# Rows for the w2-gradient tiles: five in turn, then half rows, and a new home for the second x tile

## The chip, the cores and the metric

The kernel runs on one core of a Trainium2 chip. The metric is the device time of one execution in microseconds. Three runs of the kernel before gave 1481.81, 1483.12 and 1483.87 us; the median is 1483.12 us. The engines of the core are TensorE (PE, with its weight loads PEld), VectorE (DVE), ScalarE (ACT), GpSimd (POOL) and SyncE (SP). Each works through its own list of instructions in order and waits on semaphores for the others. SyncE and GpSimd also start the transfers; a list entry that waits holds back all that stand behind it, transfers included.

## The reference

The computation is one block of a network and the gradients of all its inputs. With x of 2048 x 1024, a condition c and a modulation matrix w_mod:

```
mod = silu(c) @ w_mod                    # six rows: sa, ca, ga, sb, cb, gb
h   = layernorm(x) * (1 + ca) + sa
x   = x + ga * irfft2(rfft2(h) * (w_r + 1j*w_i))
h   = layernorm(x) * (1 + cb) + sb
x   = x + gb * (gelu(layernorm(h) @ w1 + b1) @ w2 + b2)
out, vjp = x, gradients of x, w_r, w_i, w1, b1, w2, b2, c, w_mod for grad_out
```

w1 is 1024 x 3584, w2 is 3584 x 1024, everything is stored in bfloat16, and the ten outputs are the block's value and nine gradients. The gradient of w2 (`out_6`, 3584 x 1024) is the product of the hidden activations, transposed, with the gradient that reaches the second matrix product.

## The kernel before

The two-dimensional transform is done as dense products with cosine and sine matrices that the kernel makes itself. Folding (sums and differences of mirrored rows and columns) cuts the transform into four classes CE, SE, CO and SO. The same function, `spectral_core`, serves the forward pass and the gradient: `s_fwd` makes four tiles U (products `pu`, line 471); eight `pair` steps (products `pcs`, line 504) form the spectrum, multiply it by the weights and fill R; `s_inv` makes four tiles V from R (products `pv`, line 564); and four blocks of products `po` (line 629) give the tiles `ct`, each of which is handed to `consume`.

Between the two spectral passes stand the forward products of the feed-forward part (`pp`, `pz`, `pbo`) and the gradient `pg` of its input, in four token blocks.

The part that the change touches runs from about 970 us to the end. TensorE's order there is written out by hand. A generator, `pieces()`, gives out the products of the w2 gradient (`gw2_product`, line 1073: 16 matmuls, one 128 x 512 half of a 128 x 1024 row tile, 28 row tiles `fc` in all) and then those of the w1 gradient (line 1240). `fill(n)` takes n of them. Row tiles 0 and 1 are done in the last block of the loop above, 2 to 7 are taken by `fill(2)` and `fill(10)` ahead of the spectral pass, and four halves stand beside each of the eight pairs; the rest go between the `consume` steps. Both spectral parts and fillers share the engines that empty the accumulators.

Each finished half of a w2-gradient tile is cast by whichever of VectorE and ScalarE the scheduler chooses (`nc.any`, line 1069; ScalarE for 54 of the 56) into one of the two rows of the tile `gwo`, row `fc % 2`. After the second half the row is stored by GpSimd (line 1071). So a cast of row tile `fc` waits for the store of row tile `fc - 2`. The accumulators of these products are four banks of PSUM (`ps_f`); `pu`, `pv` and part of the other spectral products have two banks (`ps_s`).

Beside the pairs run the steps of `gmod_ring` (lines 968 to 992): rows of w_mod are loaded by SyncE, reduced by VectorE (line 987), and overwritten with a row of the w_mod gradient (line 989) which GpSimd stores (line 990). Each pair loads its weights with two plain transfers (line 489) and two gathers on GpSimd (line 490) and its saved spectrum (line 492), and stores its part of the weight gradients with two plain transfers (line 550) and two scatters on GpSimd (line 551).

`consume_bwd` (line 1159) unfolds a `ct` tile, loads the matching block of x with `load_tok` (one plain transfer on SyncE, line 128, and two gathers on GpSimd, line 131), normalizes it on ScalarE (`norm_act`, line 461), and forms the gradient of x. The x tiles `xt` of the four blocks take two homes in turn (line 619), `sma` and `smb`. In both passes, `smb` also holds the matrices of CO and SO that the last two `s_inv` steps read, so the second x tile can be loaded only after those. A "home" is a tag of the pool `reg` with one buffer: a new tile of the same tag waits until the last reader of the tile before it is done. The home `gm` holds a small identity tile before the w2 products, and from pair 1 on the matrices `gm`; the home `px0` holds the pairs' evacuated tiles `cs`, and after the spectral pass of the gradient a small tile `sr`.

Ahead of the code stands only the line that sets the two homes, which the change replaces:

```
xts = [reg.tile([P, 4, D], BF16, name="xt", tag=tg)[:] for tg in ("sma", "smb")]
```

Of the kernel before, what the change touches and what calls it, by code (L numbers as in the profile page):

```python
# [11 lines left out]
BF16 = mybir.dt.bfloat16  # L12
# [5 lines left out]
P = 128  # L18
S = 2048
D = 1024  # L20
# [4 lines left out]
KH = D // 2  # L25
# [10 lines left out]
def kernel(  # L36
# [24 lines left out]
    nc = tc.nc  # L61
# [4 lines left out]
    reg = ctx.enter_context(tc.tile_pool(name="reg", bufs=1))  # L66
# [410 lines left out]
    def spectral_core(fwd, fb, sms, em, css, pt, evac_u, evac_c, evac_v, consume, o4tag, pfs=None, fill=lambda n: None, mid=lambda: None, beside=lambda n: None):  # L477
# [112 lines left out]
        for par in range(2):  # L590
            for m in range(4):
# [9 lines left out]
                if par == 0 and m > 0:  # L601
                    v = 0 if fwd else 1
                    if m == 1:
                        gm = reg.tile([P, 12, 256], BF16, name="gm", tag="gm")
# [3 lines left out]
                    else:  # L608
                        cl = (CE, SE)[m - 2]
                        for h in range(2):  # L610
                            with tc.issue_after(ld_in[0].ins):
                                nc.sync.dma_start_transpose(out=gm[:, 2 * cl:2 * cl + 2, h * P:(h + 1) * P],
                                                            in_=d_E[:, v, 2 * cl + h, :])
# [2 lines left out]
        with tc.issue_after(r_in[0].ins):  # L616
            nc.vector.tensor_scalar(out=gm[:, 8:12, :], in0=gm[:, 4:8, :], scalar1=-1.0, scalar2=None, op0=ALU.mult)
        ct = reg.tile([P, 4, 4, D], BF16, name="ct", tag=o4tag)
        xts = [reg.tile([P, 4, D], BF16, name="xt", tag=tg)[:] for tg in ("sma", "smb")]
        for i in range(4):  # L620
            o4 = ct[:, 3 * (i % 2)]
            for cl in range(4):
# [98 lines left out]
    def consume_fwd(i, o4, tmp, tmp2, x4):  # L721
# [13 lines left out]
        nc.sync.dma_start(out=chunk_rows(d_n3, i), in_=tmp)  # L735

    spectral_core(True, fbuf, (smA, smB), em1[:, 1], [css[:, 0], css[:, 1]], new_pair_temps(PXT[2:6]),
                  act_copy, act_copy, act_copy, consume_fwd, "fr")

# [185 lines left out]
    for g in range(7):  # L925
        wtile = reg.tile([P, 4, D], BF16, name=f"w1T_{g}", tag=W1T[g])
        for k in range(4):
            fc = g * 4 + k
# [127 lines left out]
        halves_sum(acc3[1], p4, b == 0, b == 3)  # L1056

    gwo = reg.tile([P, 2, D], BF16, name="gwo", tag="ph")

    def hh_of(fc):  # L1060
        return hh_f[:, fc] if fc < 2 else hh_s[hh_o[fc]]
# [3 lines left out]
                         start=(t == 0), stop=(t == NT - 1))  # L1065

    def gw2_out(acc, fc, h):
        with tc.high_priority():
            nc.any.tensor_copy(out=gwo[:, fc % 2, h * KH:(h + 1) * KH], in_=acc[:])  # L1069
        if h == 1:  # L1070
            nc.gpsimd.dma_start(out=out_6[fc * P:(fc + 1) * P, :], in_=gwo[:, fc % 2])

    def gw2_product(fc, h):
        acc = ps_f("gw2acc")
        for t in range(NT):
            gw2_mm(acc, fc, h, t)
        gw2_out(acc, fc, h)
# [122 lines left out]
    def pieces():  # L1200
# [18 lines left out]
        for fc, h, acc in last:  # L1219
            gw2_out(acc, fc, h)  # L1220
# [55 lines left out]
    def beside_bwd(n):  # L1276
        for k in range(4):
            fill(1)
            if 3 - k < (1, 2, 2, 2, 2, 2, 3, 3)[n]:
                with tc.issue_after(hh_in[0].ins):  # L1280
                    next(rows34)

    spectral_core(False, fbuf2, (smA2, smB2), em2, [css2[:, 0], css2[:, 1]],
                  new_pair_temps(["t0", "t1", "t2", "t3"]), act_copy, s_copy, act_copy, consume_bwd, "fr", pfs, fill, mid_bwd, beside_bwd)

# [55 lines left out]
```

## Time and profile before

| what | value |
|---|---|
| median of three runs | 1483.12 us |
| profiled execution: its time | 1487.43 us |
| profiled execution: its span, first to last instruction | 1485.5 us |
| TensorE busy | 1402.2 us, 94% |
| VectorE busy | 1069.0 us, 72% |
| ScalarE busy | 720.3 us, 48% |
| GpSimd busy | 362.6 us, 24% |
| mean granted TensorE clock | 0.98 of full speed |
| w2-gradient casts on ScalarE | 54, mean 583 ns |
| w2-gradient stores on GpSimd | 28 of 256 KB, median 571 ns to issue |
| `pu` products of the gradient pass | 1029.81 to 1068.43 us |
| pairs of the gradient pass, first `pcs` to first `pv` of CO | 1068.43 to 1214.27 us |

All times of instructions count from the start of the span. A line of the timeline gives start, duration, engine, line of the code, operation, the tile written and the tiles read, how many instructions were merged, and in brackets how long the engine sat idle before and what released it. A line of the waits gives who waited for whom, the total, how many times, and the longest. Engines other than the one that sets the end may be idle at no cost; what counts is the wait that ends last at each place.

### The profile page before, as it was taken

The numbers are of one execution on the slowest core, as the hardware profiler recorded it, in microseconds if no ns is written. First come the engines' busy times: TensorE is split into PE (matmuls) and PEld (weight loads), VectorE is DVE, ScalarE is ACT, GpSimd is POOL, SyncE is SP. The second block draws the span as 40 slices with busy tenths as digits, with TensorE's granted clock in tenths as the row PEclk, the third lists the DMA queues.
The fourth block names the chain that finished last, engine by engine and source line by source line (L and its number), as shares of the span: only waits on it lengthen the run. The fifth ranks groups of instructions, "written<-read, shape, count | busy, mean of one in ns | idle before, by whom it ended". The sixth has DMA issues, their size and how long they took to land.

```text
span 1485.5 us, 18204 instructions
## 1 busy us (share of the span) xinstructions
PE 1402.2 (94%) x6703; PEld 653.7 (44%) x6835; DVE 1069.0 (72%) x1574; ACT 720.3 (48%) x960; POOL 362.6 (24%) x421
## 2 busy tenths in 40 slices
PE   5889989999899999999999999997999999899998
PEld 2434545444344444444344444443444444444443
DVE  5883786898799788887420899986367677888533
ACT  4765546857886756666202333332522444453211
POOL 5620541211113122212111001112134421322323
PEclk8999999999999999999999999999999999999999
DMA  9982563899776876797898266477499977565994
GB/s 335 274 226 61 150 224 122 267 245 338 252 237 213 260 241 219 236 275 230 237 290 253 97 218 227 145 209 196 127 210 246 261 229 213 161 198 154 267 222 169
DMA packets 358046, 324.27 MB, mean 218 GB/s; under 512 B 209066, under 2 KB 300736, under 8 KB 357702
## 3 DMA queue, kind: packets, MB, share of 16 engines
q1 hardware_dynamic: 324166, 207.71, 51.9%
q0 software_dynamic: 33792, 115.40, 22.5%
q8 instruction: 53, 0.87, 0.2%
q14 instruction: 35, 0.29, 0.1%
HBM read 162.06 MB, written 111.20 MB: 184 GB/s over the span
## 4 chain that ended last, share of the span: by engine, by line
PE 32%; DVE 31%; issue 16%; DMA 9%; ACT 8%; POOL 4%; SPq 0%; POOLq 0%; DVEq 0%; ACTq 0%
PE pbo L846 9%; PE pz L797 5%; DVE ct L173 5%; DVE gt L173 4%; PE pu L471 4%; PE pg L943 3%; PE gw2acc L1064 3%; PE pv L564 3%; DVE got L1027 2%; DMA out_dram<-otl 2%; PE gw1acc L1240 1%; ACT ct L461 1%; PE pp L679 1%; DVE st L437 1%; DVE w2sA L817 1%
## 5 line engine op out<-in xcount | busy, mean ns | idle before, releaser
L679 PE MATMUL pp<-gBoT,wt 128*128 128x512 bf16 x878 | 197.4, 381 | 6.4 <-DMA wt<-in_B_w_dram 2.8
L1240 PE MATMUL gw1acc<-gzh,n3n 128*128 128x512 bf16 x876 | 195.2, 381 | 1.2 <-issue 0.2
L943 PE MATMUL pg<-w1T,gzr 128*128 128x512 bf16 x876 | 194.6, 379 | 1.6 <-ACT gn3b L951 0.2
L797 PEld LDWEIGHTS <-w 128*128 128x128 bf16 x896 | 87.6, 98 | 112.5 <-issue 9.0
L679 PEld LDWEIGHTS <-wt 128*128 128x128 bf16 x896 | 88.0, 99 | 110.8 <-issue 6.0
L1240 PEld LDWEIGHTS <-n3n 128*128 128x128 bf16 x896 | 87.7, 98 | 105.7 <-issue 2.5
L943 PEld LDWEIGHTS <-gzr 128*128 128x128 bf16 x896 | 86.8, 98 | 107.9 <-issue 4.9
L797 PE MATMUL pz<-n3Ta,w 128*128 128x512 bf16 x437 | 99.5, 383 | 6.1 <-ACT gt L800 4.1
L1064 PE MATMUL gw2acc<-gB,hhsA 128*128 128x512 bf16 x438 | 99.5, 384 | 3.4 <-DMA hhsA<-d_hh 2.1
L797 PE MATMUL pz<-n3Tb,w 128*128 128x512 bf16 x439 | 98.4, 379 | 0.5
L846 PEld LDWEIGHTS <-hhA 128*128 128x128 bf16 x608 | 59.6, 99 | 74.5 <-issue 5.8
L806 ACT ACTIVATE gt<-gt 128x2048 bf16<-128x2048 bf16 x28 | 53.5, 1910 | 70.9 <-DVE gt L173 70.9
L800 ACT ACTIVATE gt<-pz,b_col 128x512 bf16<-128x512 f32 x112 | 72.8, 684 | 29.1 <-PE pz L797 27.1
L1244 ACT CAST gwo<-gw1acc 128x512 bf16<-128x512 f32 x53 | 30.8, 584 | 115.4 <-PE gw1acc L1240 96.6
L173 DVE TENSOR_TENSOR gt<-gt,gt 128x2048 bf16<-128x2048 bf16 x56 | 68.5, 1223 | 21.6 <-ACT gt L808 20.9
L1069 ACT CAST gwo<-gw2acc 128x512 bf16<-128x512 f32 x54 | 29.9, 583 | 110.9 <-DMA out_dram<-gwo 75.6
L173 DVE TENSOR_TENSOR ct<-ct 128x2048 bf16<-128x2048 bf16 x64 | 75.8, 1219 | 10.7 <-ACT ct L632 8.8
L1064 PEld LDWEIGHTS <-hhsA 128*128 128x128 bf16 x448 | 44.0, 99 | 56.4 <-DMA hhsA<-d_hh 3.8
L987 DVE CUSTOM_DVE_ANT_0 otl<-otl 128x1024 bf16<-128x1024 bf16 x24 | 29.0, 1223 | 51.7 <-DMA otl<-in_w_mod_dram 45.3
L802 ACT ACTIVATE gt<-gt 128x2048 bf16<-128x2048 bf16 x28 | 53.4, 1907 | 0.6
L808 ACT ACTIVATE gt<-gt 128x2048 bf16<-128x2048 bf16 x28 | 53.4, 1907 | 0.5
L1245 POOL DMA_DIRECT2D out_dram<-gwo x56 | 30.7, 550 | 79.6 <-ACT gwo L1244 59.3
(313 smaller groups left out, 2508.5 us busy)
## 6 DMA issues: line engine op xcount, KB each, us to landing
gzr<-d_gz SPq DMA_DIRECT2D x28, 512.0 KB
wblk<-in_w_mod_dram SPq DMA_DIRECT2D x12, 1024.0 KB
out_dram<-otl POOLq DMA_DIRECT2D x48, 256.0 KB
d_ph<-pho POOLq DMA_DIRECT2D x21, 512.0 KB
d_hh<-hhA POOLq DMA_DIRECT2D x19, 512.0 KB
w2sD<-in_B_w_dram SPq DMA_DIRECT2D x14, 512.0 KB
hhC<-d_ph SPq DMA_DIRECT2D x14, 512.0 KB
w2sA<-d_ph SPq DMA_DIRECT2D x14, 512.0 KB
```

The costliest lines, as they stand in the source:

```text
L173: return nc.vector.tensor_tensor(out=out, in0=a, in1=b, op=op)
L471: last_pu[0] = nc.tensor.matmul(pu[:], lhsT=fb[:, i, cl, c8 * P:(c8 + 1) * P], rhs=sm[:, i, :], start=(i == 0), stop=(i == 3))
L679: last_pe[0] = nc.tensor.matmul(pp[:], lhsT=wt[:, fg % 2, cch, k * P:(k + 1) * P], rhs=gBoT[j][:, cch, :], start=(cch == 0), stop=(cch == ...
L797: last_pe[0] = nc.tensor.matmul(pz[:], lhsT=w1s[g][:, cch, k * P:(k + 1) * P], rhs=n3T[:, cch, :], start=(cch == 0), stop=(cch == NDC - 1))
L800: nc.scalar.activation(out=zb[:, k, :], in_=pz[:], func=ACT.Identity, bias=b1_col[:, fc:fc + 1], scale=1.0)
L802: nc.scalar.activation(out=av, in_=zb, func=ACT.Square)
L806: nc.scalar.activation(out=sg, in_=bv, func=ACT.Sigmoid, scale=2.0 * GK)
L808: nc.scalar.activation(out=bv, in_=bv, func=ACT.Sigmoid, scale=-2.0 * GK)
L846: last_pe[0] = nc.tensor.matmul(pbs[i][:], lhsT=hh[:, k, i * P:(i + 1) * P], rhs=wp[:, k, :], start=False, stop=(g == 6 and k == 3))
L943: last_pg[0] = nc.tensor.matmul(pgs[i][:], lhsT=gzs[b, g][:, k, i * P:(i + 1) * P], rhs=w1Ts[g][:, k, h * KH:(h + 1) * KH], start=(g == 0 ...
L1064: nc.tensor.matmul(acc[:], lhsT=hh_of(fc)[:, t, :], rhs=gBs[t // 4][:, t % 4, h * KH:(h + 1) * KH], start=(t == 0), stop=(t == NT - 1))
L1240: nc.tensor.matmul(acc[:], lhsT=n3ns[t // 4][:, t % 4, cch * P:(cch + 1) * P], rhs=gz2[t // 8][:, t % 8, :], start=(t == 0), stop=(t == NT ...
```

## The change

There are three edits. First, the row tiles 0 to 7, those ahead of the pairs, take five rows in turn instead of two: the two rows of `gwo` and three rows of a new tile `gwoE` in the home `gm`. Second, from row tile 8 on, the two rows of `gwo` stay in use, but each half is stored on its own as soon as it is cast, 128 KB each. Third, the second x tile of both spectral passes has the home `px0` in place of `smb`, so that it waits for the last pair's `cs` tile to be read instead of for the last `s_inv`.

```diff
         ct = reg.tile([P, 4, 4, D], BF16, name="ct", tag=o4tag)
-        xts = [reg.tile([P, 4, D], BF16, name="xt", tag=tg)[:] for tg in ("sma", "smb")]
+        xts = [reg.tile([P, 4, D], BF16, name="xt", tag=tg)[:] for tg in ("sma", "px0")]
...
     gwo = reg.tile([P, 2, D], BF16, name="gwo", tag="ph")
+    gwoE = reg.tile([P, 3, D], BF16, name="gwoE", tag="gm")
+    gwo5 = [gwo[:, 0], gwo[:, 1]] + [gwoE[:, k] for k in range(3)]
...
     def gw2_out(acc, fc, h):
+        row = gwo5[fc % 5] if fc < 8 else gwo[:, fc % 2]
+        half = slice(h * KH, (h + 1) * KH)
         with tc.high_priority():
-            nc.any.tensor_copy(out=gwo[:, fc % 2, h * KH:(h + 1) * KH], in_=acc[:])
-        if h == 1:
-            nc.gpsimd.dma_start(out=out_6[fc * P:(fc + 1) * P, :], in_=gwo[:, fc % 2])
+            nc.any.tensor_copy(out=row[:, half], in_=acc[:])
+        if fc >= 8:
+            nc.gpsimd.dma_start(out=out_6[fc * P:(fc + 1) * P, half], in_=row[:, half])
+        elif h == 1:
+            nc.gpsimd.dma_start(out=out_6[fc * P:(fc + 1) * P, :], in_=row)
```

The scheduler's lists of the other engines follow from it. TensorE's list is as before. GpSimd's has 20 stores more, and the gathers of the second x tile of the gradient pass stand ahead of the last pair's scatters rather than behind them. On ScalarE the four normalizations of that tile come ahead of the copies of the last 16 `pv` products rather than among the `ct` casts, and one cast of a w2-gradient half goes from ScalarE to VectorE in pair 7.

## The prediction

> **What bounds the kernel now.** I read the page's busy shares first, then TensorE's waits from 960 us on, where the changed code runs, and then ScalarE, GpSimd and VectorE in order of time at the places those waits named. TensorE is busy 94% of the span; the change leaves its order of instructions as it is, so the change can only remove or add TensorE waits. The page, then TensorE's waits:
>
> ```profile
> span 1485.5 us, 18204 instructions
> PE 1402.2 (94%) x6703; PEld 653.7 (44%) x6835; DVE 1069.0 (72%) x1574; ACT 720.3 (48%) x960; POOL 362.6 (24%) x421
> ```
>
> ```profile
> PE pu L471 <- ACT U L642: 7.7, 1, 7.7
> PE po L629 <- DVE ct L632: 7.3, 2, 5.3
> PE pv L564 <- ACT V L642: 2.1, 1, 2.1
> PE gw2acc L1064 <- DMA hhsA<-d_hh: 2.1, 1, 2.1
> PE gw2acc L1064 <- ACT gwo L1069: 0.9, 2, 0.7
> ```
>
> The longest is one wait of 7.7 us for ScalarE to empty a bank of `pu`, at 1031.65 to 1039.34. ScalarE, GpSimd and TensorE there:
>
> ```profile
> 1037.73 1.07 ACT L1069 CAST gwo<-gw2acc 128x512 bf16<-128x512 f32 x2 [14.20 <-DMA out_dram<-gwo]
> 1038.69 1.09 ACT L642 CAST U<-pu 128x512 bf16<-128x512 f32 x2
> ...
> 1026.09 0.54 POOL L990 DMA_DIRECT2D out_dram<-otl  x1 [15.54 <-DVE otl L989]
> 1035.12 0.58 POOL L1071 DMA_DIRECT2D out_dram<-gwo  x1
> ...
> 1039.34 0.59 PE L471 MATMUL pu<-smA,fbuf 128*128 128x512 bf16 x1 [7.69 <-ACT U L642]
> ```
>
> The casts of tile row 7 wait for row 5's store, because both use row 1 of `gwo`; that store stands on GpSimd behind a w_mod-gradient store that waits for VectorE; and the `U` copies stand behind the casts on ScalarE. Now the place where the second `xt` comes in:
>
> ```profile
> 1198.76 4.64 ACT L461 ACTIVATE xt<-xt,stats 128x1024 bf16<-128x1024 bf16 x4 [12.72 <-DMA xt<-in_A_x_dram,xu]
> 1236.05 1.24 ACT L461 ACTIVATE xt<-xt,stats 128x1024 bf16<-128x1024 bf16 x1 [4.43 <-DMA xt<-in_A_x_dram,xu]
> ...
> 1207.29 1.30 DVE L173 TENSOR_TENSOR Pt<-cs01b 128x1028 bf16<-128x1028 bf16 x2 [1.93 <-ACT cs01b L645]
> 1237.79 9.54 DVE L173 TENSOR_TENSOR ct<-ct 128x2048 bf16<-128x2048 bf16 x8 [4.32 <-ACT ct L632]
> ...
> 1193.18 1.03 POOL L131 DMA_INDIRECT xt<-in_A_x_dram,xu  x1 [0.31 <-issue]
> 1229.58 1.02 POOL L131 DMA_INDIRECT xt<-in_A_x_dram,xu  x1 [0.30 <-PE po L629]
> ```
>
> The second x tile is gathered only at 1229.58, when `smb` is free; its normalization stops ScalarE 4.43 us, and the last `ct` cast behind it holds VectorE back 4.32 us. The pair stage between (1068 to 1214 us) is set by VectorE waiting for transfers, by VectorE's list of waits from 1068 to 1230:
>
> ```profile
> DVE otl L987 <- DMA otl<-in_w_mod_dram: 31.6, 10, 7.6
> DVE Pt L173 <- ACT cs01b L645: 17.6, 2, 15.7
> ```
>
> **The change, part by part.**
>
> *Five rows until the pairs.* Rows 5, 6 and 7 of the products now wait for the stores of rows 0, 1 and 2. These were issued by 999.84, and row 7's casts come at about 1030, so nothing waits. ScalarE then empties `pu` as it is filled, as it does from 1050 on (a copy every 0.87 us). U's 128 matmuls at 14.0 us per 64 (1054.60, 13.99 us) plus 0.55 us of column sums are 28.5 us; the stage takes 38.6 us now (1029.81 to 1068.43). That removes 10.1 us: 7.7 of wait, 0.2 of a second gap, and 2.2 of matmuls at a clock of 0.50 from 1036 to 1044. What is late next: VectorE's last fold of `fbuf` ends at 1031.5, in step with the first group, and the pairs' first inputs (`ws`, issued by 1034) are there. The first pair then starts at 1058.3.
>
> The rows' new home is `gm`, which the pairs load at 1076.67 (1066.6 shifted). Row 7's store leaves GpSimd by 1047.95 and GpSimd stores let their row go 2.6 to 4.3 us after issue (1035.12 to 1037.73, 1113.11 to 1117.37): 14 us of cover, cost nothing.
>
> *Half rows from row 8 on.* 20 rows give 20 more GpSimd DMAs at 0.57 us, 11.4 us, on an engine busy 51 of 130 us in the pair stage; one now stands between the two `ws` gathers of a pair, and one before the outgoing scatters. What it can win is TensorE's 0.7 and 0.2 us for `gwo`, the 2.1 for `hhsA` with 1.7 of slow clock, and 2.1 for `V` behind a cast: at most 6.8 us. What it can cost is 2 x 0.57 us in each of 8 pairs, 9 us, if GpSimd's queue were the chain. I take nothing from either: pair 7's `R` ends at 1215.6 while TensorE's first `pv` of CO starts at 1214.27, so VectorE's pairs set the end of the stage. Their loop (stores of one pair's `pf`, next `otl` load, 4 to 7 us landing, two reductions, 9.9 us of pair) contains no `gwo` store; as cs of pairs 1 to 6 was waiting for VectorE, a later or earlier cast moves nothing there. So all of this stage moves 10.1 us forward with its first `cs`.
>
> *Second x tile in px0, backward.* The gather now waits for VectorE to have read pair 7's `cs`, not for the last `pv`. In the new order GpSimd issues it after pair 6's scatters and two stores, and ScalarE normalizes it, and makes two `gwo` casts, ahead of the 16 copies of `V`. In times of before, with t = 0 where pair 7's `cs` is complete (1207.25):
> - VectorE has read `cs` at 1.3; GpSimd reaches the gather at 2.0. From gather to first normalization the trace has 5.6, 6.5, 4.9 and 5.6 us; I take 5.6: 7.6.
> - four normalizations 4.6 (1198.76), two casts 1.1, the first `V` copy 0.6: bank free at 13.9.
> - TensorE: `R` comes at 8.4 (0.6 later than before, for one `gwo` cast that VectorE now makes before it); two banks of `pv` are full at 9.5. It waits 4.4 us.
> - After TensorE's waits of 2.09 (1140.4) and 5.32 us (1261.6) the granted clock was at half for 3.4 us: 1.7 us lost. After the 2.14 us one it stayed at 1.00. For 4.4 us I take 1.7.
> - So `po` starts at 9.5 + 4.4 + 14 groups x 0.875 + 1.7 = 27.85; before it was at 21.07 (1228.32): 6.8 us later.
> - Against that, VectorE's 4.3 us before its unfold go: the `ct` cast no longer has a normalization ahead of it.
>
> The unfold thus starts 2.5 us later than before, relative to pair 7. TensorE's 5.3 us wait at 1261.6 shrinks to about nothing, but its later waits for `po` (1.05 at 1300, 1.95 at 1341.8) are behind VectorE's work on the x tiles, and grow by as much: +2.5. Bounds: if the gather lands in 4.9 us and the clock holds, +0.1; at 6.5 with 3.4 us of slow clock lost, +5.1.
>
> The Trainium skill, "TensorE: Matmul & The Clock Gate", section "What's actually happening", has the clock fall after an idle window of about 3.4 us that runs free of the kernel. By it a 4.4 us wait always throttles, and 1.7 us is the least it costs; the trace agrees only in part, since 2.09 us was enough once and 2.14 was not. By the skill the sum would be the same or up to 1.7 us worse.
>
> *The same in the forward pass, and after.* The second x tile comes earlier there, but VectorE has no wait for `xt` in that stage, and the weight group loaded last (366.51) is now group 6 instead of 5, needed later: nothing. `sr` now waits in px0 for the last add on the fourth x tile (1384.56 to 1386.83), 4.2 us after ScalarE's turn at 1382.61; four accumulators of 3.45 us stand in front of TensorE, and VectorE reads `sr` at 1390.20: nothing. From 1346.84 on TensorE runs without a wait to 1479.10, so what is gained by then reaches the end.
>
> **Sum.** -10.1 + 2.5 = -7.6 us. It is made against the profiled execution, 1487.43 us (span 1485.5 and 1.9 outside it), which is 4.3 above the median of the runs; I take the difference from the median: 1483.1 - 7.6 = 1475.5.
>
> **Rivals.**
> - *The wait before V does not come* (0.15). For it: an x load that lands under 5 us, as at 1274.18; against it, three of four took longer, and the order puts the normalization first. Then the unfold starts 0.6 - 4.3 = 3.7 us earlier: 1483.1 - 13.8 = 1469.3.
> - *The pair stage keeps what it is given* (0.20). VectorE's w_mod-gradient work up to 1050.9 follows transfers that do not move, the DMA share is already 0.9 to 1.1 from 1085 to 1185, and the extra issues sit in GpSimd's queue. For it: 31.6 us of VectorE's waits there are for transfers; against: 1065 to 1080 has a share of 0.25, room to move into. Half of the 10.1 returned gives 1480.5, all of it 1485.6.
> - *Slower than before* (0.10): the early gather is late. It stands behind pair 6's scatters on GpSimd, which wait for SyncE's stores (12.2 and 8.3 us as the longest). Each us of delay keeps `V`'s copies and TensorE 1 us longer. At 7.6 us more, a gather that lands 13 us after t = 2, the gain is gone; at 10.6 more it is 0.2% slower; with a 12 us wait 1487.5. Against: at this place the scatters of before waited 0.3 us.
> - *Nothing moves* (0.03): row 7 waits for another store. Row 2's store was issued 30 us earlier, so hardly.
>
> **How the numbers follow.** The forecast has 0.52. A difference of 0.2%, 3.0 us, is about what a measurement of this kernel can tell. Faster by more: 0.50 of the forecast, 0.15 of the first rival, 0.10 of the second: 0.75. Within: 0.14. Slower: 0.11, the late gather and the rest of the second. The range runs from the first rival, 1469, to short of the whole gain's return, 1482.5: 0.05 below it, 0.15 above. The forecast's own range by its bounds is 1473 to 1478.
>
> **What the profile after would show.** The 7.7 us wait of `pu` is gone and the first `pcs` comes 10 us earlier; casts of `gwo` no longer wait for stores before 1040; TensorE waits 3 to 6 us at the third `pv` of CO for a copy of `V`, and ScalarE's four normalizations of the second x tile stand just ahead; VectorE's 4.3 us before the unfold is gone. The forecast is wrong if the first `pcs` is early but the first `pv` of CO is not, or if that wait is over 8 us.

## The result and the profile after

The changed kernel takes 1489.92 us (median of six runs, 1486.81 to 1493.34) against 1482.84 us for the kernel before on the same chip (six runs, 1481.66 to 1484.93): the ratio is 1.0051, with a 95% interval of 1.0036 to 1.0065. It is 7 us slower, where 7.6 us faster was forecast. It lies on the side of the third rival, the early gather that is late.

The profiled execution of the changed kernel took 1486.81 us. TensorE's waits from 1000 us on, most costly first (total, times, longest):

```profile
span 1484.7 us, 18247 instructions
PE pv L564 <- ACT V L642: 13.7, 2, 13.5
PE gw1acc L1246 <- DMA gzh<-d_gz: 2.3, 1, 2.3
PE po L629 <- DVE ct L632: 2.2, 2, 1.8
PE po L629 <- ACT ct L632: 2.0, 1, 2.0
```

The 7.7 us wait of `pu` is gone, and TensorE's 5.3 us for VectorE in `po` as well. One wait of 13.5 us has taken their place: TensorE at the `pv` products, for a copy of `V`. In order of time, ScalarE first (a cast of row 7, which no longer waits for a store, and the first copy of `U`; then the place of the new wait), GpSimd's two gathers of the second x tile, SyncE's queue beside them, and TensorE:

```profile
1022.90 0.58 ACT L1073 CAST gwoE<-gw2acc 128x512 bf16<-128x512 f32 x1 [2.86 <-PE gw2acc L1066]
1027.17 0.58 ACT L642 CAST U<-pu 128x512 bf16<-128x512 f32 x1 [0.22 <-PE pu L471]
...
1200.54 2.37 ACT L461 ACTIVATE xt<-xt,stats 128x1024 bf16<-128x1024 bf16 x2 [10.31 <-DMA xt<-in_A_x_dram,xu]
1209.16 2.37 ACT L461 ACTIVATE xt<-xt,stats 128x1024 bf16<-128x1024 bf16 x2 [6.25 <-DMA xt<-in_A_x_dram,xu]
1211.44 1.04 ACT L1073 CAST gwo<-gw2acc 128x512 bf16<-128x512 f32 x2
1212.38 1.08 ACT L642 CAST V<-pv 128x512 bf16<-128x512 f32 x2
...
1192.42 2.00 POOL L131 DMA_INDIRECT xt<-in_A_x_dram,xu  x1 [0.30 <-DMA out_dram<-gwo]
1194.72 1.39 POOL L131 DMA_INDIRECT xt<-in_A_x_dram,xu  x1 [0.30 <-issue]
...
1193.56 0.38 SPq L1231 DMA_DIRECT2D n3n<-d_n  x1
1194.03 9.25 SPq L1208 DMA_TRANSPOSE otl<-d_hh  x1
...
1054.41 1.91 PE L504 MATMUL pcs<-empf,U 128*128 128x256 bf16 x16
1196.81 0.81 PE L564 MATMUL pv<-smB,R 128*128 128x512 bf16 x3
1213.02 14.59 PE L564 MATMUL pv<-smB,R 128*128 128x512 bf16 x55 [13.48 <-ACT V L642]
...
1231.93 9.54 DVE L173 TENSOR_TENSOR ct<-ct 128x2048 bf16<-128x2048 bf16 x8
```

Read upward from TensorE's line: it stands from 1199.54 to 1213.02, because the first two `V` copies come at 1212.38; these stand behind two casts, these behind four normalizations of the second x tile, and the last two of those waited for a gather that was issued at 1194.72 and was in place only at 1209.16, 14.4 us later. VectorE's unfold starts without its 4.3 us wait, as the change allows, but the `po` it needs are late.

The clock and the transfers at that place, in four steps of 4 us (start and end, length, busy time of TensorE, its loads, VectorE, ScalarE, GpSimd, granted clock, share of the DMA engines, GB/s):

```profile
1196.00:1200.00 4.00, 2.88 (x13) 1.04 (x12) 4.00 (x7) 0.00 (x0) 1.28 (x3) 1.00 1.02 345
1200.00:1204.00 4.00, 0.00 (x0) 0.00 (x0) 1.91 (x4) 2.37 (x2) 0.54 (x1) 0.59 1.33 112
1204.00:1208.00 4.00, 0.00 (x0) 0.00 (x0) 0.00 (x0) 0.00 (x0) 0.00 (x0) 0.50 1.23 109
1208.00:1212.00 4.00, 0.00 (x0) 0.00 (x0) 0.00 (x0) 2.84 (x4) 0.00 (x0) 0.50 1.07 270
```

From 1200 to 1208 no engine computes for most of the time, and the DMA engines are full (1.33 and 1.23) while they move a third of what they moved just before. The clock is granted at half from 1200.7 to 1217.8.

By stages, from the first instruction of each to the next (us; all these are profiled executions):

| stage | before | changed |
|---|---|---|
| `pu` to first `pcs` (U stage) | 38.8 | 28.3 |
| first `pcs` to first `po` (pairs and `V`) | 159.9 | 173.0 |
| first `po` to the end of the last | 118.7 | 117.9 |
| from there to the end of the last `gw1acc` | 132.1 | 131.4 |
| from there to the end of the span | 6.3 | 7.9 |

The U stage gives 10.5 us and the two stages behind the pairs 1.5; the pairs with `V` take 13.1 and the end 1.6: +2.7 in all. The two spans differ by -0.8 because before's profiled execution reached its first `pu` at 1029.60 and this one at 1026.11; in the thirteen profiles of this study that start lies between 1026.1 and 1032.9, with and without any of the edits. The medians differ by 7.1 us: the changed kernel's profiled execution was the shortest of its six, 3.1 below their median, and that of the kernel before, 1487.43 us, lay 4.6 above its own. Which part is longer in the executions without a profile was not seen, so the stages explain the direction of the change and 2.7 of its 7.1 us.

### The profile page after: what moved, and what is told of

The parts are those of the page before. It is cut to its first block, busy times and chain, and to the rows that moved or that the text cites. A ratio compares the mean times of both kernels' runs of the same rounds, so it can differ in the third digit from the quotient of the medians.

```text
span 1484.7 us, 18247 instructions
## 1 busy us (share of the span) xinstructions
PE 1398.6 (94%) x6703; PEld 653.6 (44%) x6835; DVE 1069.5 (72%) x1575; ACT 720.6 (49%) x959; POOL 375.2 (25%) x441
## 4 chain that ended last, share of the span: by engine, by line
PE 45%; DVE 29%; issue 9%; ACT 7%; DMA 6%; POOL 3%; SPq 0%; POOLq 0%; DVEq 0%; ACTq 0%
PE gw2acc L1066 9%; PE pbo L846 9%; PE gw1acc L1246 6%; PE pg L943 6%; PE pz L797 5%; DVE ct L173 4%; DVE gt L173 4%; PE pu L471 4%; PE pv L564 3%; DVE got L1027 2%; ACT ct L461 1%; DVE gn3a L1032 1%; DVE st L437 1%; DVE w2sA L817 1%; PE pp L679 1%
## 5 line engine op out<-in xcount | busy, mean ns | idle before, releaser
L173 DVE TENSOR_TENSOR ct<-ct 128x2048 bf16<-128x2048 bf16 x64 | 75.9, 1220 | 5.2 <-ACT ct L632 3.9
L1073 ACT CAST gwo<-gw2acc 128x512 bf16<-128x512 f32 x45 | 25.7, 582 | 91.1 <-PE gw2acc L1066 66.8
```

Of the source, the lines that this page charges most:

```text
L173: return nc.vector.tensor_tensor(out=out, in0=a, in1=b, op=op)
```

## The experiments

The stage lengths of all kernels, in us, each from its profiled execution (U stage; first `pcs` to first `po`; `po`; last store's issue to the end), with the one wait for `V` at the end of the pairs, and the ratio to the kernel before:

| kernel | U | to `po` | `po` | end | wait for `V` | ratio, 95% interval |
|---|---|---|---|---|---|---|
| before | 38.8 | 159.9 | 118.7 | 5.33 | 0 | 1 |
| changed | 28.3 | 173.0 | 117.9 | 6.96 | 13.5 | 1.0051 [1.0036, 1.0065] |
| five rows alone | 28.4 | 159.9 | 119.8 | 5.33 | 0 | 0.9927 [0.9901, 0.9954] |
| five rows, half rows | 28.7 | 158.6 | 122.3 | 6.96 | 0 | 0.9959 [0.9942, 0.9977] |
| px0 alone | 38.7 | 169.4 | 117.4 | 5.33 | 8.1 | 1.0067 [1.0042, 1.0093] |
| five rows, px0 | 28.7 | 166.8 | 118.7 | 5.33 | 4.9 | 1.0018 [1.0008, 1.0029] |
| changed, late normalization | 28.9 | 159.7 | 115.2 | 6.97 | 0 | 0.9946 [0.9928, 0.9965] |
| five rows, px0, late normalization | 28.3 | 158.0 | 119.1 | 5.33 | 0 | 0.9932 [0.9920, 0.9944] |
| changed, two transposed loads left out | 28.5 | 169.4 | 117.3 | 6.96 | 6.9 | 1.0024 [1.0011, 1.0037] |
| changed, `n3n` later | 28.3 | 173.7 | 121.5 | 6.96 | 8.2 | 1.0057 [1.0041, 1.0073] |
| changed, both of these | 28.3 | 166.9 | 123.2 | 6.96 | 5.4 | 1.0023 [1.0002, 1.0044] |
| five rows, half rows from row 18 | 28.3 | 158.4 | 118.8 | 6.14 | 0 | 0.9952 [0.9931, 0.9973] |
| five rows, all rows in halves | 28.3 | 159.5 | 119.6 | 8.06 | 0 | 0.9983 [0.9958, 1.0009] |

**The parts one by one.** Five rows alone is the changed kernel with these two undone:

```diff
-        xts = [reg.tile([P, 4, D], BF16, name="xt", tag=tg)[:] for tg in ("sma", "px0")]
+        xts = [reg.tile([P, 4, D], BF16, name="xt", tag=tg)[:] for tg in ("sma", "smb")]
...
-        if fc >= 8:
-            nc.gpsimd.dma_start(out=out_6[fc * P:(fc + 1) * P, half], in_=row[:, half])
-        elif h == 1:
+        if h == 1:
```

> Only the five rows in turn for the first eight rows; whole rows stored throughout, second x tile back in the home smb. Theory 1 (the late gather of the second x tile, ahead of the V copies on ScalarE, took the gain): the U stage is about 10 us shorter as in the changed kernel (first pcs some 28 us after the first pu, against 38.6), no V wait of 13 us appears, and 6 to 10 us of it stay: 1473 to 1477 us, ratio 0.993 to 0.996. Theory 2 (the half rows, twelve more stores on GpSimd's queue, crowd the transfers of the end): the same here, because no half row is stored. Theory 3 (the pairs and the backward pass wait for another thing and take up any gain): the U stage is shorter but the end is within 2 us of before, ratio 0.999 to 1.001.

It measured 1475.27 us against 1485.91, ratio 0.9927: 10.6 us faster. Theories 1 and 2 both expected it (theory 2 counts twelve more stores; there are twenty); the third, that the pairs take the gain back, falls.

The second keeps the half rows and undoes only the first of the two lines above.

> Five rows and half rows, second x tile back in the home smb. Theory 1: the half rows cost nothing or save up to 3 us, so 1470 to 1477 us, ratio 0.991 to 0.996, no V wait. Theory 2: the half rows cost what the five rows brought, so about 1483 us or above, ratio 0.999 to 1.005, with the 4096-byte packets of the gathers slow around the end of the pairs although the second x tile is elsewhere. Theory 3: as for the five rows alone.

1479.92 us, ratio 0.9959: 6 us faster. It lies at the slow end of what theory 1 expected of the ratio (its time is over the 1477 us expected), so the half rows are not what made the changed kernel slower than before, but they cost something against five rows alone. The intervals overlap a little; the profiles say where: 1.3 us are gained before `po`, 2.5 are lost in `po`, and 1.6 at the end (below).

The third is the kernel before with one word changed:

```diff
-        xts = [... for tg in ("sma", "smb")]
+        xts = [... for tg in ("sma", "px0")]
```

> The kernel before with nothing changed but the home of the second x tile (px0). Theory 1: its two normalizations that stand ahead of the V copies wait for their gather, TensorE waits some 6 to 14 us for V, and the kernel is 3 to 12 us slower: ratio 1.002 to 1.008. Theory 2: without half rows the gather lands in 5 to 6 us, the V wait is about 4 us and the kernel is within 3 us of before: ratio 0.999 to 1.002.

1495.46 us against 1485.91, ratio 1.0067: 10 us slower, as theory 1 expected. Its ScalarE and TensorE at the place:

```profile
1214.37 2.37 ACT L461 ACTIVATE xt<-xt,stats 128x1024 bf16<-128x1024 bf16 x2 [6.53 <-DMA xt<-in_A_x_dram,xu]
1218.97 2.37 ACT L461 ACTIVATE xt<-xt,stats 128x1024 bf16<-128x1024 bf16 x2 [2.23 <-DMA xt<-in_A_x_dram,xu]
...
1222.84 14.53 PE L564 MATMUL pv<-smB,R 128*128 128x512 bf16 x55 [8.09 <-ACT V L642]
```

The same picture with no half row stored: the second gather, issued at 1208.79, is in place at 1218.97, 10.2 us later, and TensorE waits 8.1 us. Five rows and the new home are thus a gain of about 10 us and a loss of about 10; with the half rows the wait is longer still and the end too, and the sum is a loss.

The fourth keeps all three parts, and the early gather, and moves only the normalization of the second x tile on ScalarE, behind the first LayerNorm activation of the first x tile:

```diff
-        nc.scalar.activation(out=tmp, in_=n_ap, func=ACT.Identity, scale=sc[:, 3:4], bias=sc[:, 2:3])
+        ln_in.append(nc.scalar.activation(out=tmp, in_=n_ap, func=ACT.Identity, scale=sc[:, 3:4], bias=sc[:, 2:3]))
...
-        norm_act(n1, n1, 0, i)
+        with tc.issue_after(ln_in[-4].ins) if i == 1 else ExitStack():
+            norm_act(n1, n1, 0, i)
```

> The changed kernel with all three parts, but the normalization of the second x tile is queued on ScalarE behind the first backward LayerNorm activation of the first x tile, and so behind all V copies; its gather is issued as early as before. Theory 1: the 13 us wait of TensorE for V goes, po begins 10 us or more earlier than in the changed kernel, and the five rows' gain returns: 1470 to 1477 us, ratio 0.991 to 0.996, though the gather still takes 10 to 15 us to land. Theory 2 (the crowded transfers themselves cost the time, whoever waits first): the V wait goes but another wait for a transfer takes its place, 1483 to 1490 us, ratio 0.999 to 1.005.

1476.54 us, ratio 0.9946: 8 us faster than before, and some 15 faster than the changed kernel, which has the same instructions but for one cast, on VectorE there and on ScalarE here. ScalarE at that place:

```profile
1205.41 0.59 ACT L1075 CAST gwo<-gw2acc 128x512 bf16<-128x512 f32 x1 [2.87 <-PE gw2acc L1068]
1206.47 0.59 ACT L642 CAST V<-pv 128x512 bf16<-128x512 f32 x1 [0.47 <-PE pv L564]
...
1240.57 1.23 ACT L461 ACTIVATE xt<-xt,stats 128x1024 bf16<-128x1024 bf16 x1
```

`V` is copied as it comes, and TensorE's first wait after 1195 us that is over 1 us is 2.1 us for `gzh`. The transfers are crowded here too: from 1210 to 1214 us the DMA engines are full (1.03) at 107 GB/s. It is the order on ScalarE that cost the time; theory 2, that the crowded transfers cost it whoever waits, falls.

**Why the gather is late.** Two things stand on SyncE's queue beside it: the 1 MB loads of `n3n` and the transposed loads of `hh`. Each was taken away by itself; the kernel without the two transposed loads leaves those rows of the w2 gradient without their operands, and its time serves the question alone.

```diff
-            if 6 <= fc + 2 < NFC:
+            if 6 <= fc + 2 < NFC and fc + 2 not in (25, 26):
```

> The changed kernel without the two transposed loads of hh for the rows 25 and 26 (their products take what lies in those buffers, so these rows of the w2 gradient are not the reference's); in the changed kernel these loads stand on SyncE's queue at 1194.03 and 1206.43. Theory A (the transposed loads beside the gather make it late): the second piece of the gather is there 5 to 8 us after its issue instead of 14.4, the wait for V is 3 to 6 us, about 1478 to 1482 us, ratio 0.995 to 0.999. Theory B (the 1 MB loads of n3n ahead of them are what the gather stands in): the gather still takes 10 us or more, the V wait stays at 9 to 14 us, ratio 1.000 to 1.005.

```diff
-            nc.sync.dma_start(out=n3n[:], in_=chunk_rows(d_n3, b))
+            with tc.issue_after(hh_in[0].ins):
+                nc.sync.dma_start(out=n3n[:], in_=chunk_rows(d_n3, b))
```

> The changed kernel with the four loads of n3n queued on SyncE behind the last transposed load of hh, so that the transposed loads of rows 25 and 26 are alone beside the gather. Theory A: the second piece of the gather still takes 10 us or more and TensorE waits 9 to 14 us for V; 1484 to 1492 us, ratio 1.000 to 1.006 (the first product of the w1 gradient may wait some us for n3n on top). Theory B: the gather takes 5 to 8 us, the V wait is 3 to 6 us, ratio 0.994 to 0.999 less what the later n3n costs.

Without the two transposed loads the wait for `V` is 6.9 us, ratio 1.0024; with `n3n` later it is 8.2 us, ratio 1.0057. The latter holds a wait of 8.9 us for `gzh`, 2.3 in the changed kernel, and one of 5.0 us for a cast at 1130 us; the first comes behind the later `n3n`, the second was not looked into. Neither theory's numbers came out whole. In both the four normalizations run in one piece, so that the second piece of the gather is there at most 7.9 us after its issue without the transposed loads, as theory A expected, and at most 9.2 with `n3n` later; but the first piece is slow too (7.8 and 9.2 us), either edit alone takes 5 to 7 of the 13.5 us, and neither brings the wait to the 3 to 6 us expected of the guilty one. TensorE in the two, in that order:

```profile
1215.65 14.80 PE L564 MATMUL pv<-smB,R 128*128 128x512 bf16 x56 [6.92 <-ACT V L642]
```

```profile
1217.27 14.42 PE L564 MATMUL pv<-smB,R 128*128 128x512 bf16 x56 [8.21 <-ACT V L642]
```

So both were taken away together, in the changed kernel.

> The changed kernel with neither the transposed loads of rows 25 and 26 (their products take what lies in the buffers) nor the early loads of n3n (queued behind the last transposed load): the gather of the second x tile has SyncE's queue quiet beside it. If the lateness is the sum of both crowds, the second piece is normalized within 5 to 6.5 us of its issue, as the prediction took it, and TensorE waits 4 to 5 us for V. If the wait for V stays at 7 us or more though the piece is there in time, the rest of it is ScalarE's own work ahead of the V copies. The w1 gradient's first product waits for its operands again, some 9 us, so the time says little: ratio 1.000 to 1.005.

```profile
1198.72 1.41 POOL L131 DMA_INDIRECT xt<-in_A_x_dram,xu  x1 [0.30 <-issue]
...
1202.83 4.63 ACT L461 ACTIVATE xt<-xt,stats 128x1024 bf16<-128x1024 bf16 x4 [8.61 <-DVE R L173]
1208.31 1.06 ACT L642 CAST V<-pv 128x512 bf16<-128x512 f32 x2
...
1208.94 14.07 PE L564 MATMUL pv<-smB,R 128*128 128x512 bf16 x56 [5.41 <-ACT V L642]
```

All four normalizations run in one piece, as the prediction took it: the two gathers of the tile land 6.2 and 4.6 us after their issue, at 1202.72 and 1203.36 (the line names `R`, but the wait ends with the first landing). The wait is 5.4 us, a little over the 4 to 5 expected, and from the first `pv` of CO to `po` it takes 22.0 us. Against 14.05 in the kernel before that is 8.0 us; the forecast's step said 6.8. The ratio is 1.0023, with a wait of 8.3 us for `gzh` in it that comes behind the later `n3n`.

The third thing beside the gather is the half rows' stores. With whole rows throughout (the second line of the first diff undone alone):

> The changed kernel with whole rows stored throughout: five rows and the second x tile in px0. If the half rows add to the lateness of the gather, the V wait is 8 to 11 us as in the kernel with only the new home, and the time about 1482 to 1486 us, ratio 0.998 to 1.001; if they do nothing, 1488 to 1492 us, ratio 1.003 to 1.006, with a V wait of 13 us.

1488.35 us, ratio 1.0018: between the two expectations, and below the changed kernel's interval. The wait for `V` is 4.9 us, smaller than expected of either. So any one of the three, transposed loads, `n3n` or half rows, may go and the wait falls from 13.5 to between 5 and 8 us. How much each is worth can't be told from one profile of each: px0 alone (8.1) and five rows with px0 (4.9) have the same transfers there and differ by 3.2.

The records of the DMA packets show the crowding itself. In the changed kernel, from 1200 to 1210 us, the 256-byte packets of the transposed loads take 44 to 165 ns on average (by steps of 2 us) and the 4096-byte packets of GpSimd's queue, the gather's and its stores' alike, 270 to 550; from 1190 to 1192 it was 18 and 166. With the transposed loads left out, the 4096-byte packets keep to 159 to 166 ns from 1200 to 1212. But the gather is not what slows the transposed loads: from 1204 to 1206 us their packets take 59 ns with five rows alone and 126 with half rows as well, while no 4096-byte packet starts beside them, as the gathers of the second x tile start only at 1217.5 and 1219.6 us there. So the new home moved the gather into a stretch that can be slow without it (in the kernel before, from 1214 to 1220 us, the same loads' packets take 18 to 23 ns). What makes it slow was not found.

The Trainium skill, "DMA: Bandwidth & Descriptors", section "Issuing engines are not separate DMA queues", says that transfers started by SyncE and GpSimd run on the same 16 DMA engines and interleave. The trace agrees in that packets of both lie side by side, 491 of the transposed loads and 28 of GpSimd's queue from 1204 to 1206 us. The Trainium skill, "Advanced Engine Details and Errata", section "X-Bar Transpose (TRN2)", says that transposing DMAs are as fast as regular ones. The traces do not bear that out: with `n3n` later, transposed loads alone fill the engines (1.11) at 226 GB/s from 1198 to 1200 us, where the changed kernel's plain loads reach 376 at 1.07 from 1214 to 1216; and at the place of the late gather it was 109 to 112, against 345 just before.

**All good parts together.** Five rows, whole rows, px0, and the late normalization:

> Five rows, whole rows, second x tile in px0 with its normalization behind the V copies. If the half rows cost some 3 to 5 us whoever waits, this is 3 us faster than the same kernel with half rows: 1470 to 1474 us, ratio 0.990 to 0.993, with the 4 to 5 us of VectorE's wait in the backward pass gone beside the 10 us of the U stage. If the half rows cost nothing here, ratio 0.994 to 0.996.

1475.85 us, ratio 0.9932. The half rows' 3 us and the 4 to 5 us of VectorE can't be seen in the times: the interval overlaps that of the same kernel with half rows (0.9946), and five rows alone is as fast (0.9927). The new home brings nothing even when its normalization is out of the way. Five rows alone is the version to keep; it beats both kernels by one edit.

**The end of the span.** All kernels with half rows end later after their last store. Half rows from row 18 on, and for all rows, on five rows with the second x tile in smb:

```diff
-        if fc >= 8:
+        if fc >= 18:
```

> Five rows, second x tile in smb, half rows stored singly from row 18 on alone: ten stores more than with whole rows instead of twenty. From the last store's issue to the end of the span it is 5.33 us in all kernels with whole rows and 6.96 us in those with twenty half rows more; if this goes by the number of stores on GpSimd's queue, 6.1 to 6.2 us here; if it is a step, 5.33 or 6.96 us. The time: 1474 to 1480 us.

```diff
-        if fc >= 8:
+        if fc >= 0:
```

> Five rows, second x tile in smb, half rows for all 28 rows: 28 stores more than with whole rows. By the number of stores the end of the span lies 7.6 us behind the last store's issue; if it is a step, 6.96 us. The time: 1477 to 1483 us, as with half rows from row 8 on.

The last store is issued at 1464.99 us of a span of 1471.1 in the first, and at 1467.29 of 1475.3 in the second:

```profile
1464.99 0.54 POOL L1251 DMA_DIRECT2D out_dram<-gwo  x1 [2.91 <-ACT gwo L1250]
```

```profile
1467.29 0.54 POOL L1251 DMA_DIRECT2D out_dram<-gwo  x1 [2.91 <-ACT gwo L1250]
```

That is 5.33 us with no store more, 6.14 with ten, 6.96 with twenty and 8.06 with 28. It goes by the number of stores, 0.082 us each up to twenty; the last eight cost 0.137 each, more than expected. The times are 1474.05 us, ratio 0.9952, and 1478.46, ratio 0.9983, both within what was expected: with all rows in halves most of the gain of the five rows is gone in the time, though the stages to `po` are as long as in the others.

## Why the prediction was wrong

*Five rows.* Right in mechanism and size. 10.1 us were forecast for the U stage (38.6 to 28.5 us), 10.5 came (38.8 to 28.3; the kernel before starts its first `pu` at 1029.60, not at 1029.81), in every kernel with five rows between 9.9 and 10.5, and alone they make the kernel 10.6 us faster. The second rival, that the pairs return the gain, is refuted: with five rows alone the stage behind stays 159.9 us long.

*The second x tile in px0: the step that failed.* Its place, its order on ScalarE and the chain gather, four normalizations, two casts, `V` were as forecast; one term was not, "from gather to first normalization ... I take 5.6". The 5.6 was measured from the first of the tile's two gathers to the first normalization, and the four normalizations were then taken as one piece. By that measure the changed kernel has 8.1 us (1192.42 to 1200.54), and its normalizations come in two pieces: from the second gather's issue to the two that need it, it was 14.4 us, where the four tiles of before have 6.2 to 7.9. With t = 0 where pair 7's `cs` is complete (1189.8 in the changed kernel), the gather started at 2.6 (forecast 2.0), the normalizations ended at 21.7 (12.2), and the first `V` copy at 23.2 (13.9): 9.3 us late. TensorE's wait was 13.5 us instead of 4.4, 9.1 more. The half clock behind it cost 2.4 us, half of 1213.02 to 1217.8, instead of 1.7. First `pv` of CO to `po` grew from 14.05 us (1214.27 to 1228.32) to 30.6 (1196.81 to 1227.44): 16.6, where 6.8 + 9.1 + 0.7 is 16.6. The quiet kernel puts the blame on that one term: without the transposed loads and `n3n` beside the gather, the same stretch grew by 8.0 us for a forecast of 6.8, with a wait of 5.4 us for 4.4. The whole stage from the first `pcs` to `po` grew by 13.1 only, because the pairs up to the first `pv` of CO took 142.4 us instead of 145.8 (144.0 to 148.5 in the other kernels); what shortened them is open.

Where the 5.6 came from explains the error. It was the median of four gathers of before; those run beside SyncE's queue at other places. The new place, just behind the last pair, is where SyncE starts 1 MB loads of `n3n` and two transposed loads, and the prediction counted nothing of what stands beside the gather there. It did name this case as a rival and put its break-even at a landing of 13 us, but gave it a tenth, from the wait of GpSimd's scatters ahead of the gather; those did wait only 0.3 us. It was the transfer that was late, not its issue (2.6 us for 2.0). The prediction's own test, "the forecast is wrong ... if that wait is over 8 us", caught it.

*VectorE's 4.3 us.* They went, as said, but the `po` stage shrank by 0.8 us only (118.7 to 117.9). With the normalization late it shrank by 3.5, to 115.2. In both, 2.1 to 2.3 us of the gain went into a new wait of the first `gw1acc` for `gzh`, whose transposed loads start 21.0 us after the first `po` as in the kernel before, while what stands ahead of that product became shorter. The prediction named no such wait.

*Half rows, costed at nothing.* Wrong by about 3 us in the profiles, inside the bounds of -6.8 and +9. They did remove most of a wait for `V` behind a cast in the middle of the pairs, at 1158 us (3.5 us with five rows alone, 0.8 with half rows), and `po` comes 1.3 us sooner; but the second x tile's gather came no earlier against the `pcs`, and TensorE's wait for VectorE in `po` grew from 4.9 to 7.7. The end of the span, 1.6 us, was in no step.

*The clock.* The forecast took 1.7 us from a 3.4 us half clock. The Trainium skill, "TensorE: Matmul & The Clock Gate", section "What's actually happening", has it fall after an idle window of about 3.4 us. The trace agrees only in part: in the 13.5 us wait it fell to half at 1200.7, 1.2 us after the wait began, and it stayed there until 4.8 us after its end. That a 4.4 us wait always throttles, as the prediction has it, does not follow from that section, since a window that runs free of the kernel need not fit into it whole. It is what was measured all the same: from 1000 to 1470 us in the thirteen profiles, half clock came during or just behind each of TensorE's 21 waits of 3.2 us and more, and 12 of the 20 waits of 2.0 to 2.9 us.

## What to carry to other kernels

A transfer's landing time belongs to the place where it runs: list what stands on the other queues in the same microseconds before taking a median from elsewhere. An early transfer is of use only if nothing that waits for it stands in an in-order queue ahead of work that is due sooner; here moving four activations behind the copies turned 7 us lost into 8 us gained. And test the parts of a change singly: one edit of the three held all of the gain.

## What was unexpected of the hardware

- Each store more on GpSimd's queue lengthens the end of the span, though the last of the stores more was issued over 200 us before it: 5.33, 6.14, 6.96 and 8.06 us from the last store's issue to the end with 0, 10, 20 and 28 stores more. In each of the kernels with whole rows it is 5.33, in each with twenty more it is 6.96 or 6.97. The time lies in an instruction `DRAIN` on GpSimd that is recorded beside the last store: it lasts 4.56 us with no store more, 5.38 with ten, 6.19 with twenty and 6.85 with 28, 0.082 us a store throughout. The remaining 0.4 us with 28 stores comes behind it. What `DRAIN` waits for was not seen.
- Transposed loads at times become slow, and what runs beside them too: 109 GB/s with full DMA engines, 256-byte packets up to 165 ns against 18, 4096-byte packets up to 550 against 166. It does not take a gather (59 and 126 ns in the two kernels named above), and it did not happen each time that both ran: at 1228 to 1230 us in the kernel before, the transposed loads' packets took 18 ns and those of GpSimd's queue 167 within the same 2 us. What tells the two apart stays open.
